# A new issue order, other PSUM banks and other engines for the same 1680 steps of a linear-attention and FFN kernel

## The chip, the cores and the metric

The kernel runs on one core of a Trainium2 chip. The core has a matrix engine (TensorE: PE in the profile, its weight loads PEld), a vector engine (VectorE: DVE), a scalar engine (ScalarE: ACT), GpSimd (POOL) and SyncE (SP). Here POOL and SP mostly issue DMAs, and sixteen DMA engines carry them out. Each engine works through its own instruction stream in order and waits on semaphores for the others. The metric is the device time of one launch in microseconds (us), the median of several runs. Times in the profile count from the first instruction.

## The reference

Inputs are `q`, `k`, `v` of 8 batches x 8 heads x 576 rows x 64, a feature matrix `w_phi` (64x128), and FFN weights `moe_w_in` (512x2048) and `moe_w_out` (2048x512), all float32.

```python
def phi(x):
    proj = np.einsum('bhsd,df->bhsf', x, w_phi)
    proj = proj - np.max(np.abs(proj), axis=-1, keepdims=True)
    return np.concatenate([np.exp(proj), np.exp(-proj)], axis=-1)
q_p, k_p = (phi(q), phi(k))
kv = np.einsum('bhsf,bhsd->bhfd', k_p, v)
z = np.sum(k_p, axis=2)
num = np.einsum('bhsf,bhfd->bhsd', q_p, kv)
den = np.einsum('bhsf,bhf->bhs', q_p, z)[..., None] + 1e-06
attn = num / den
...
h = np.maximum(x @ w_in, 0.0)      # x: attn as 4608 rows of 512
out = h * h @ w_out
```

There is no softmax over positions: each head has a small matrix `kv` (256 x 64), with which every query row is multiplied.

## The kernel before, in words

The work goes batch by batch. For each of the 8 batches the attention makes 576 rows of `x`: 512 of them are one block of the FFN, and the last 64 of all batches together make a ninth block (tile `xS`). The FFN of a block is a first matmul (`F1`, L788: x tile by `win`, 16 groups of four 128x512 matmuls), relu and square (L765 or L767, then L774), and a second matmul (`F2`, L882: by `wout`, four row groups, each in four parts of four matmuls), then a copy out of PSUM (`ot`, L193 or L195) and a store. The attention of the next batch is mixed into the FFN of the present one.

The attention of one batch consists of these steps:
- loads of k, q and v by POOL (L249, L257, L269, L278), which also turn float32 into bf16;
- transposes of k and q into `kT` and `qT`: on PE for batches 0 and 1 (L320), from batch 2 on by a transposing DMA of SP (L331);
- projections `Pk` and `Pq` (L347; 64-row matmuls), their largest magnitude (`Mk` L405, `Mq` L498 or L531) on VectorE, and the exponentials on ScalarE (`kp`, `kn` L411; `qf` L544 or `qpn` L584);
- from batch 3 on the q features are turned by a transposing DMA of SP (`Xf`, L548); before that a matmul `Fq` (L569) makes them turned;
- `V` (L428, VectorE) scales v, `KVs` and `KV` (L450, L462) build kv on PE, `kvc` copies it to SBUF;
- per group of 128 rows: `NA` (L648, PE), `SA` (L660, VectorE, scales the half sum), `NB` (L648 again), `rd` (L670, reciprocal), `xo` (L674, VectorE, into a ring of three buffers), and `Xx` (L708), a transposing DMA of SP that makes the x tile `xT` or `xS` which F1 reads.

The program first makes a plan of 1680 numbered steps. A step is a closure that issues one or several instructions on one engine. The lists at the end of the file then say how the steps are issued:
- `ORDER` is the sequence of all steps. `pin` chains each engine's instructions in that sequence, so each engine does its steps in the order in which they stand there.
- `BASES` gives each of the 377 uses of PSUM its bank (0 to 7). A step that opens a bank waits until all readers of the bank's former use are through.
- `STATES` says for 233 steps (relu, `ot`, `kvc` and some copies in the head) whether they run on their first engine or on the other of VectorE and ScalarE.
- `GATES` makes a load of batches 2 and up wait for a named step.
- `FILL` puts matmuls of zeros (L961, "warm") ahead of a step: its number, then bank and count.

```python
    def arrange(self):
        for op in self.ops:
            if op.alt is not None and STATES[op.group] == "1":
                op.eng, op.occ, op.lat = op.alt
        for g, b in zip(self.banks, BASES):
            g.base = int(b)
        return [self.ops[i] for i in ORDER]
...
        if now[0].seq in GATES:
            dep(i, plan.ops[GATES[now[0].seq]].ins, mybir.DependencyClass.Sync)
```

The costs and slacks in the upper part of the file (`act_cost`, `SLACK`, `LD`) have no effect on what is issued: the four lists and `GATES` alone set it.

Steps that are named below, with their line, and their time in the profiled execution:
- head: 0 and 1 load a first piece of k by ACT's queue, 7 and 8 cast it (L193, L195; 2.84 and 3.56), 2 loads w_phi, 3 and 4 cast it (L230; 3.24 on), 5 sets the identity's tile to zero (L238; 3.10), 11 on POOL makes the identity of it (L913; 3.77), 40 is the first transposes (L320; 4.16), 41 their copy, 42 the first projection; 12 to 39 are loads, 22 to 25 win, 36 to 39 wout
- 358 (last load of batch 2's k), 373 and 374 (its kT and qT, SP L331; 49.91 and 54.54), 266, 275, 284 and 293 (the four x tiles of batch 1, SP L708; from 59.33 on), 292 (xo; 64.02), 297 (NA; 64.77), 482 (first F1 of block 1; 70.86)
- 425 and 604 (Pq), 465 (Fq), 441 to 446 (NA, SA, NB, rd, xo, Xx; 446 at 96.58), 755 (kT of batch 4), 608 (Xf), 455 and 464 (Xx; 103.33 and 106.08), 665 and 669 (F1 of block 2)
- 659 and 661 (NA and NB; 145.5), 838 to 842 (SA, NB, rd, xo, Xx; 842 at 173.16), 1081 (ot; 171.59), 990 and 1002 (Xf), 1137 (kT of batch 6; 181.19), 1022 (Pq), 972 (KVs), 1139 (Pk; 187.81)
- 1028 and 1030 (NA, NB), 1156 (Mk; 206.75), 1033 (Xx; 208.83), 1238 (first F1 of block 5; 214.7)
- 1425 (NB; 280.7), 1427 (xo), 1428 (Xx, the last part of xS; 289.95), 1585 (F1 of the ninth block; 300.8), 1666 to 1673 (last F2, in halves, L846), 1674 and 1675 (their copies), 1676 to 1679 (their stores, by SP and ACT)

Of the kernel before, what the change touches and what calls it, by code (L numbers as in the profile page):

```python
# [108 lines left out]
def kernel(  # L109
# [858 lines left out]
    2, 0, 1, 13, 14, 12, 8, 6, 7, 5, 3, 4, 11, 19, 40, 41, 9, 42, 46, 48, 10, 74, 66, 47, 75, 15, 67, 76, 45, 43, 18,  # L968
    68, 44, 77, 17, 71, 58, 88, 16, 90, 59, 70, 89, 26, 91, 27, 60, 78, 69, 92, 20, 49, 80, 81, 79, 28, 50, 61, 21,
    93, 51, 94, 30, 72, 52, 54, 98, 63, 57, 95, 22, 99, 64, 131, 65, 73, 53, 23, 55, 62, 83, 24, 156, 82, 132, 25,  # L970
    157, 29, 56, 133, 101, 38, 85, 128, 102, 84, 109, 86, 34, 212, 87, 110, 103, 213, 36, 111, 129, 214, 37, 112,
    104, 113, 105, 100, 215, 130, 33, 194, 158, 106, 195, 218, 108, 107, 216, 188, 219, 96, 114, 189, 121, 97, 115,
    134, 217, 122, 200, 206, 135, 116, 123, 207, 124, 159, 117, 125, 201, 136, 118, 126, 160, 190, 137, 127, 119,
    191, 120, 142, 161, 138, 145, 143, 220, 146, 307, 308, 221, 147, 139, 311, 312, 309, 144, 233, 162, 313, 303,
    140, 163, 304, 223, 148, 141, 164, 149, 322, 305, 222, 165, 310, 150, 166, 319, 323, 306, 151, 315, 314, 320,
    152, 196, 316, 198, 321, 167, 317, 153, 197, 325, 154, 199, 318, 328, 168, 326, 169, 155, 324, 170, 174, 329,
    208, 171, 356, 186, 175, 331, 330, 35, 187, 209, 176, 184, 39, 245, 332, 334, 246, 32, 185, 173, 177, 234, 31,
    172, 340, 335, 178, 361, 211, 327, 202, 359, 179, 203, 341, 477, 360, 210, 481, 365, 180, 181, 204, 357, 242,
    336, 346, 225, 243, 224, 355, 205, 485, 358, 247, 342, 347, 236, 363, 182, 267, 226, 276, 362, 268, 352, 183,
    235, 337, 269, 364, 227, 366, 192, 277, 489, 353, 549, 193, 338, 278, 237, 254, 238, 373, 255, 239, 490, 348,  # L980
    244, 248, 241, 258, 240, 249, 228, 259, 229, 230, 270, 260, 231, 374, 285, 333, 343, 271, 232, 339, 261, 344,
    272, 262, 495, 286, 263, 499, 250, 287, 264, 273, 265, 503, 274, 266, 354, 294, 251, 295, 507, 252, 275, 256,
    296, 279, 508, 513, 280, 253, 257, 551, 345, 288, 281, 547, 289, 349, 282, 556, 283, 290, 379, 350, 284, 375,
    553, 382, 517, 291, 376, 744, 531, 292, 377, 367, 381, 293, 297, 535, 370, 298, 378, 369, 380, 521, 552, 299,
    351, 422, 548, 387, 300, 423, 539, 389, 546, 525, 301, 557, 390, 371, 543, 526, 388, 554, 438, 544, 413, 550,
    482, 439, 414, 372, 486, 440, 563, 483, 416, 368, 424, 484, 383, 487, 429, 417, 747, 478, 430, 555, 564, 474,
    488, 431, 384, 740, 492, 475, 479, 476, 391, 504, 395, 392, 385, 500, 493, 404, 505, 518, 406, 501, 302, 494,
    396, 522, 386, 506, 502, 510, 397, 523, 527, 405, 565, 480, 415, 496, 394, 524, 519, 540, 497, 511, 393, 514,
    498, 398, 532, 491, 515, 407, 754, 545, 541, 516, 419, 559, 447, 533, 420, 399, 400, 749, 448, 401, 741, 534,
    408, 449, 582, 512, 739, 409, 403, 402, 410, 562, 583, 536, 411, 737, 421, 412, 432, 520, 585, 668, 561, 433,  # L990
    738, 537, 528, 418, 584, 742, 434, 672, 435, 748, 529, 436, 558, 574, 538, 437, 425, 456, 577, 542, 722, 746,
    426, 457, 560, 575, 726, 934, 428, 458, 441, 730, 442, 743, 576, 530, 443, 604, 444, 427, 734, 445, 607, 446,
    450, 605, 465, 676, 466, 755, 467, 451, 680, 606, 735, 452, 570, 681, 453, 566, 454, 704, 572, 567, 686, 608,
    609, 571, 568, 459, 569, 708, 745, 460, 573, 616, 461, 586, 455, 619, 690, 462, 463, 587, 468, 618, 712, 509,
    469, 464, 578, 617, 470, 580, 694, 620, 471, 472, 716, 581, 628, 579, 640, 631, 698, 736, 621, 589, 665, 630,
    756, 588, 683, 699, 629, 596, 666, 673, 595, 717, 677, 674, 682, 632, 667, 590, 678, 641, 591, 633, 592, 684,
    669, 593, 594, 935, 598, 701, 937, 670, 473, 597, 642, 687, 679, 931, 671, 675, 945, 610, 688, 695, 611, 643,
    689, 691, 752, 685, 696, 612, 943, 702, 705, 613, 692, 614, 750, 765, 703, 706, 599, 936, 652, 693, 600, 767,
    707, 723, 928, 697, 653, 768, 939, 719, 724, 932, 655, 766, 601, 720, 753, 713, 603, 938, 654, 602, 757, 769,
    714, 751, 758, 622, 645, 731, 658, 930, 623, 759, 859, 715, 933, 760, 732, 771, 624, 634, 656, 625, 709, 635,  # L1000
    626, 863, 710, 770, 644, 636, 727, 711, 877, 733, 728, 637, 638, 772, 867, 729, 718, 721, 700, 807, 725, 761,
    615, 881, 764, 885, 809, 639, 762, 871, 808, 947, 763, 889, 872, 646, 810, 895, 647, 890, 795, 773, 797, 627,
# [105 lines left out]
```

## Time and profile before

| what | value |
|---|---|
| median of 3 runs | 345.33 us (344.21 to 345.71) |
| profiled execution: own time | 346.37 us |
| profiled execution: span | 344.6 us |
| granted TensorE clock, mean | 0.998 |
| busy: PE, DVE, ACT, POOL | 333.8, 269.2, 221.6, 95.5 us |
| DMA, mean over the span | 149 GB/s, 51.51 MB |
| matmuls F2 (L882) and F1 (L788), busy | 127.7 and 104.7 us (L788 from `xS`: another 15.3) |
| fillers (L961) | 128 matmuls, 11.1 us busy |

The profiled execution is one run of the program, recorded by the hardware. Its own time is longer than its span by what lies ahead of the first and behind the last recorded instruction. A row of a timeline has the start, the duration, engine, line, operation, the tiles written and read, the shape and the number of instructions; in brackets stands how long the engine was idle before it, and what ended that. "SPq" rows are the issues of DMAs on SP: their duration is that of the issue, and the transfer lands later. Matmuls are pipelined: one of 512 columns takes 379 ns from start to end, but they follow each other every 0.216 us.

### The profile page before, as it was taken

To read this page: it belongs to the slowest core of one execution; us is meant where nothing else is said; L and a number is where in the kernel's file an instruction comes from. 1 tells how busy PE (TensorE), PEld (TensorE's weight loads), DVE (VectorE), ACT (ScalarE), POOL (GpSimd) and SP (SyncE) were. 2 spreads that over 40 slices of the span, in tenths; PEclk is the share of its full clock that TensorE was granted. 3 is DMA by queue.
4 is the path that set the end of the run, shared out by engine and by line. 5 is a ranking of instruction groups with operands and counts; after the bars stand their busy time and mean duration, and the time that the engine had idled before them with its cause. 6 is when DMAs were issued, how large, how long until landed. Compare 5 with 4: busy or idle time off the path is not lost.

```text
span 344.6 us, 8417 instructions
## 1 busy us (share of the span) xinstructions
PE 333.8 (97%) x3371; PEld 189.0 (55%) x3402; DVE 269.2 (78%) x490; ACT 221.6 (64%) x388; POOL 95.5 (28%) x143
## 2 busy tenths in 40 slices
PE   8999999799998999999999999999999999999995
PEld 7789776445554554545545554555555454444443
DVE  5999998799888798888869987798978748861540
ACT  5999996499898787577887896886376201111101
POOL 8760571952910480104604061330000000000000
PEclk9999999999999999999999999999999999999999
DMA  9999999999999999999999999999964631101115
GB/s 135 176 205 202 201 131 157 181 154 210 128 165 195 197 169 197 177 182 185 193 178 178 170 195 168 214 151 171 199 123 92 135 90 54 47 0 62 31 58 126
DMA packets 142935, 51.51 MB, mean 149 GB/s; under 512 B 111472, under 2 KB 138416, under 8 KB 142896
## 3 DMA queue, kind: packets, MB, share of 16 engines
q1 hardware_dynamic: 97488, 32.35, 51.8%
q0 software_dynamic: 44960, 18.23, 46.3%
q8 instruction: 26, 0.43, 0.6%
q10 hardware_dynamic: 448, 0.39, 0.4%
q14 instruction: 13, 0.11, 0.1%
HBM read 36.73 MB, written 9.44 MB: 134 GB/s over the span
## 4 chain that ended last, share of the span: by engine, by line
PE 86%; DVE 5%; DMA 5%; issue 2%; ACT 1%; POOL 1%; SPq 0%; DVEq 0%; POOLq 0%
PE psum L882 31%; PE psum L788 30%; PE psum L648 5%; PE psum L462 5%; PE psum L347 5%; DMA xT<-xo 3%; PE psum L827 2%; DMA kT<-xk 2%; DVE mk L405 2%; PE psum L813 1%; PE psum L799 1%; PE psum L569 1%; PE psum L846 1%; PE psum L320 1%; PE psum L450 1%
## 5 line engine op out<-in xcount | busy, mean ns | idle before, releaser
L882 PE MATMUL psum<-wout,h 128*128 128x512 bf16 x529 | 127.7, 379 | 1.7 <-issue 0.3
L788 PE MATMUL psum<-xT,win 128*128 128x512 bf16 x448 | 104.7, 379 | 1.0 <-DMA xT<-xo 1.0
L765 ACT ACTIVATE hr<-psum 128x512 bf16<-128x512 f32 x95 | 54.9, 601 | 47.9 <-DVE h L774 28.8
L882 PEld LDWEIGHTS <-h 128*128 128x128 bf16 x560 | 51.3, 98 | 56.7 <-issue 0.3
L788 PEld LDWEIGHTS <-win 128*128 128x128 bf16 x512 | 47.4, 98 | 53.6 <-DMA xT<-xo 1.4
L774 DVE TENSOR_TENSOR h<-hr 128x512 bf16<-128x512 bf16 x144 | 56.6, 415 | 10.6 <-ACT hr L765 10.2
L544 ACT ACTIVATE qf<-psum 128x1024 bf16<-128x1024 f32 (+1 forms) x50 | 45.6, 937 | 8.6 <-PE psum L347 6.1
L405 DVE TENSOR_REDUCE mk<-psum 128x8 f32<-128x1024 f32 (+1 forms) x38 | 42.3, 1119 | 4.0 <-ACT kn L411 1.9
L411 ACT ACTIVATE kn<-psum 128x1024 bf16<-128x1024 f32 (+1 forms) x38 | 36.0, 947 | 12.8 <-PE psum L347 11.1
L411 ACT ACTIVATE kp<-psum 128x1024 bf16<-128x1024 f32 (+1 forms) x38 | 35.6, 948 | 8.2 <-PE psum L347 6.6
L767 DVE TENSOR_SCALAR hr<-psum 128x512 bf16<-128x512 f32 x49 | 33.1, 684 | 9.0 <-PE psum L788 8.2
L660 DVE TENSOR_TENSOR psum<-psum,en 128x520 f32<-128x520 f32 (+1 forms) x39 | 27.2, 703 | 10.4 <-PE psum L648 6.1
L648 PEld LDWEIGHTS <-qpn 128*128 128x128 bf16 x624 | 27.0, 97 | 15.0 <-issue 3.3
L269 POOL DMA_DIRECT2D xq<-in_q_dram x24 | 17.3, 727 | 56.3 <-issue 14.0
L531 DVE TENSOR_REDUCE mq<-psum 128x8 f32<-128x1024 f32 (+1 forms) x25 | 27.8, 1113 | 6.5 <-PE psum L347 3.9
L648 PE MATMUL psum<-kv,qpn 128*128 128x65 bf16 x624 | 30.2, 193 | 1.9 <-DVE xo L674 1.7
L249 POOL DMA_DIRECT2D xk<-in_k_dram x27 | 19.9, 740 | 30.6 <-ACT en L508 15.3
L584 ACT ACTIVATE qpn<-psum 128x1024 bf16<-128x1024 f32 (+1 forms) x30 | 27.0, 956 | 1.8 <-PE psum L569 1.8
L674 DVE TENSOR_TENSOR xo<-psum,rden 128x512 bf16<-128x512 f32 (+1 forms) x39 | 26.3, 684 | 2.4 <-DMA xT<-xo 1.8
L195 ACT ACTIVATE ot<-psum 128x512 f32<-128x512 f32 x18 | 10.8, 598 | 25.7 <-PE psum L882 25.7
L249 POOL DMA_DIRECT2D xv<-in_v_dram x27 | 19.8, 740 | 14.6 <-PE psum L788 11.7
L428 DVE TENSOR_TENSOR va<-xv,va 128x1280 bf16<-128x1280 bf16 (+2 forms) x34 | 23.2, 710 | 0.0
(79 smaller groups left out, 352.8 us busy)
## 6 DMA issues: line engine op xcount, KB each, us to landing
out_dram<-ot SPq DMA_DIRECT2D x32, 256.0 KB, 3.0
xk<-in_k_dram POOLq DMA_DIRECT2D x25, 128.0 KB, 5.1
xq<-in_q_dram POOLq DMA_DIRECT2D x24, 128.0 KB, 5.1
xv<-in_v_dram POOLq DMA_DIRECT2D x24, 128.0 KB, 5.1
win<-in_moe_w_in_dram POOLq DMA_DIRECT2D x4, 512.0 KB, 10.7
wout<-in_moe_w_out_dram POOLq DMA_DIRECT2D x4, 512.0 KB, 15.5
xq<-in_q_dram POOLq DMA_DIRECT2D x4, 256.0 KB, 6.1
out_dram<-ot SPq DMA_DIRECT2D x6, 128.0 KB, 2.4
```

The costliest lines, as they stand in the source:

```text
L249: pin(nc.gpsimd.dma_start(out=x[:, m0 + a * 512 : m0 + z * 512].rearrange("p (h x) -> p h x", x=4 * D), in_=src[b][2 * a : 2 * z, 0:512, : ...
L405: pin(nc.vector.tensor_reduce(out=mk_view(g), in_=ps2(pj)[:, :, : n * Fd].rearrange("p e (i f) -> p e i f", f=Fd), axis=AX.X, op=ALU.max, ...
L411: pin(nc.scalar.activation(out=dst[slot][:, :, :n, :].rearrange("p e i f -> p e (i f)"), in_=ps2(pj)[:, :, : n * Fd], func=ACT.Exp, scale= ...
L531: pin(nc.vector.tensor_reduce(out=mqb[:, c, :, :n], in_=ps2(pj)[:, :, : n * Fd].rearrange("p e (i f) -> p e i f", f=Fd), axis=AX.X, op=ALU ...
L544: pin(nc.scalar.activation(out=o, in_=i_, func=ACT.Exp, scale=sgn))
L648: pin(nc.tensor.matmul(out=o[:, u // 4, u % 4 * D1 : (u % 4 + 1) * D1], lhsT=qpn[slot][:, sg * half + u * m : sg * half + u * m + P], rhs= ...
L660: pin(nc.vector.tensor_tensor(out=o, in0=o, in1=enb[:m, c, :].rearrange("t (b h) -> t b h", b=2).to_broadcast([m, 2, 4, D1]), op=ALU.mult))
L765: pin(nc.scalar.activation(out=hr[sl], in_=ps1(g), func=ACT.Relu))
L767: pin(nc.vector.tensor_scalar(out=hr[sl], in0=ps1(g), scalar1=0.0, scalar2=None, op0=ALU.max))
L774: pin(nc.vector.tensor_tensor(out=dst, in0=i_, in1=i_, op=ALU.mult))
L788: pin(nc.tensor.matmul(out=o, lhsT=win[mc // 4][:, kc, mc % 4 * P : (mc % 4 + 1) * P], rhs=x, start=(kc == 0), stop=(kc == KC - 1)))
L882: pin(nc.tensor.matmul(out=ps1(g), lhsT=h2[c % 2][mc // 4][:, mc % 4, tt * P : (tt + 1) * P], rhs=wout[mc // 4][:, mc % 4, :], start=(mc = ...
```

## The change

The plan of steps, their code and `GATES` stay as they are. `ORDER`, `BASES`, `STATES` and `FILL` get other contents:
- `ORDER`: the steps are permuted, mostly by a few places. SP's sequence (113 DMAs) is the same in both. POOL's differs only among the loads 18 to 38: the loads of win come in the order 24, 23, 22, 25 rather than 22, 23, 24, 25, those of wout as 36, 37, 38, 39 rather than 38, 36, 37, 39, and 29 goes behind 36; some small loads change places.
- `STATES`: 78 of 233 steps change their engine, 42 from VectorE to ScalarE and 36 the other way (43 relus, 18 copies `ot`, 15 copies `kvc`, and one each of `kcast` and `Cxq`).
- `BASES`: 314 of 377 uses of PSUM get another bank.
- `FILL`: 89 filling matmuls instead of 128; the 23 ahead of step 101, the 9 ahead of 51 and others go, some are spread otherwise.

The diff, with the lines in which the steps named above stand:

```diff
--- before.py
+++ after.py
 ORDER = [
-    2, 0, 1, 13, 14, 12, 8, 6, 7, 5, 3, 4, 11, 19, 40, 41, 9, 42, 46, 48, 10, 74, 66, 47, 75, 15, 67, 76, 45, 43, 18,
...
-    93, 51, 94, 30, 72, 52, 54, 98, 63, 57, 95, 22, 99, 64, 131, 65, 73, 53, 23, 55, 62, 83, 24, 156, 82, 132, 25,
-    157, 29, 56, 133, 101, 38, 85, 128, 102, 84, 109, 86, 34, 212, 87, 110, 103, 213, 36, 111, 129, 214, 37, 112,
...
-    553, 382, 517, 291, 376, 744, 531, 292, 377, 367, 381, 293, 297, 535, 370, 298, 378, 369, 380, 521, 552, 299,
...
-    426, 457, 560, 575, 726, 934, 428, 458, 441, 730, 442, 743, 576, 530, 443, 604, 444, 427, 734, 445, 607, 446,
-    450, 605, 465, 676, 466, 755, 467, 451, 680, 606, 735, 452, 570, 681, 453, 566, 454, 704, 572, 567, 686, 608,
...
-    469, 464, 578, 617, 470, 580, 694, 620, 471, 472, 716, 581, 628, 579, 640, 631, 698, 736, 621, 589, 665, 630,
...
-    669, 593, 594, 935, 598, 701, 937, 670, 473, 597, 642, 687, 679, 931, 671, 675, 945, 610, 688, 695, 611, 643,
...
-    648, 1128, 913, 649, 650, 929, 798, 899, 774, 651, 777, 917, 796, 786, 657, 811, 776, 659, 903, 660, 775, 921,
-    779, 778, 907, 780, 799, 925, 788, 831, 926, 781, 661, 782, 832, 873, 783, 946, 860, 908, 784, 800, 833, 785,
...
-    977, 988, 1080, 991, 962, 839, 1081, 1062, 840, 841, 1104, 1063, 842, 848, 998, 956, 1001, 952, 1108, 953, 990,
...
-    1060, 1047, 980, 968, 849, 1126, 851, 1051, 1048, 1130, 971, 1013, 852, 1116, 1127, 1049, 1052, 1134, 1065, 1117,
...
-    1139, 1022, 1074, 972, 1025, 973, 979, 974, 1091, 1023, 976, 1142, 1069, 1082, 975, 1140, 1024, 1100, 1095, 1075,
...
-    1424, 1530, 1425, 1566, 1534, 1570, 1516, 1501, 1517, 1519, 1502, 1426, 1552, 1535, 1503, 1513, 1427, 1520, 1509,
-    1514, 1553, 1505, 1510, 1515, 1554, 1571, 1531, 1506, 1428, 1511, 1541, 1507, 1532, 1536, 1523, 1518, 1555, 1524,
...
-    1561, 1568, 1612, 1569, 1529, 1577, 1546, 1585, 1578, 1547, 1573, 1557, 1579, 1563, 1574, 1596, 1586, 1616, 1564,
...
-    1647, 1657, 1664, 1648, 1666, 1649, 1668, 1650, 1670, 1651, 1658, 1672, 1667, 1674, 1669, 1671, 1673, 1676, 1677,
...
+    2, 0, 1, 13, 14, 7, 12, 8, 6, 3, 4, 5, 11, 19, 40, 41, 9, 42, 47, 48, 10, 66, 74, 46, 67, 15, 75, 45, 68, 43, 17,
...
+    51, 20, 72, 52, 73, 94, 30, 54, 63, 95, 57, 131, 24, 99, 56, 53, 23, 64, 55, 65, 82, 81, 156, 132, 22, 128, 157,
+    25, 62, 36, 83, 101, 133, 34, 85, 109, 102, 84, 212, 29, 87, 110, 86, 103, 213, 111, 37, 129, 214, 158, 113, 38,
...
+    517, 377, 291, 292, 744, 382, 531, 376, 293, 367, 381, 297, 521, 370, 298, 378, 369, 380, 535, 552, 299, 351,
...
+    457, 575, 441, 560, 726, 458, 934, 730, 442, 743, 576, 443, 604, 444, 445, 607, 465, 676, 446, 466, 605, 450,
...
+    578, 586, 690, 617, 580, 620, 470, 717, 694, 471, 609, 472, 581, 628, 640, 631, 698, 579, 736, 669, 756, 629,
+    595, 665, 670, 699, 673, 666, 596, 630, 598, 677, 682, 621, 588, 642, 632, 683, 667, 678, 671, 590, 641, 674,
...
+    903, 907, 799, 659, 831, 660, 781, 782, 661, 783, 662, 788, 925, 785, 873, 832, 784, 908, 946, 860, 663, 834,
...
+    839, 988, 1062, 840, 841, 1081, 956, 1063, 842, 998, 952, 1000, 1104, 953, 990, 977, 1086, 1001, 957, 1090, 979,
...
+    1134, 852, 1125, 1048, 1073, 853, 1053, 1013, 1136, 854, 1077, 1061, 855, 1074, 1065, 1078, 1049, 1014, 1022,
+    1066, 972, 1139, 973, 1142, 1067, 974, 1025, 1140, 1069, 1141, 1023, 1091, 1082, 1015, 1070, 1100, 976, 1087,
...
+    1548, 1516, 1552, 1517, 1509, 1501, 1510, 1553, 1511, 1570, 1502, 1554, 1423, 1505, 1424, 1513, 1425, 1514, 1527,
+    1426, 1506, 1541, 1528, 1507, 1537, 1503, 1427, 1519, 1428, 1559, 1520, 1534, 1521, 1545, 1535, 1529, 1523, 1536,
+    1515, 1518, 1538, 1531, 1539, 1546, 1585, 1547, 1555, 1524, 1571, 1639, 1556, 1525, 1532, 1594, 1542, 1533, 1549,
...
+    1657, 1664, 1667, 1647, 1648, 1666, 1649, 1668, 1650, 1670, 1651, 1658, 1672, 1669, 1674, 1671, 1673, 1676, 1677,
...
 ]
 BASES = (
-    '1455230076225145762234566476424460160675235573406256700052456706030226636000051065454425544316464174'
...
+    '6577674402105660622234544776027640120422067175676462540072457642204004626222261062736606141516020635'
...
 )
 STATES = (
-    '0100000001011000110001110010000100000000100011110000100100001010000000101000100000000000001011010001'
-    '1010110000001000010000010001110100000000001111000000000100011000011010001011011000101110111101101011'
-    '111111100001100010101111001011011'
+    '1100000001011000100001110011010100000000100011100100110000001010000000010110000100000000001000000100'
+    '0100101101000000011010011011010000010100000111010001000100000000010110000100001101000000000000111111'
+    '101000110110110110111110101110000'
 )
...
 FILL = {
-    40: (0, 26), 42: (0, 11), 74: (0, 5), 76: (0, 7), 58: (0, 10), 60: (4, 16), 92: (4, 1), 51: (6, 9), 131: (4, 8),
-    156: (3, 2), 101: (3, 23), 188: (4, 3), 134: (2, 1), 142: (5, 6),
+    40: (0, 26), 42: (0, 11), 66: (0, 5), 68: (2, 7), 58: (4, 10), 60: (7, 7), 92: (7, 7), 131: (1, 7), 156: (7, 2),
+    109: (4, 1), 142: (5, 6),
 }
```

6 lines of the change are left out of this document (3 added, 3 removed), and 130 rows, old and new, of the table ORDER.

## The prediction

> **What bounds the kernel now.** I read the page first, then TensorE's waits, then busy time by stretches of the span, and last the timelines of PE, DVE and SP around each place where PE stood idle.
>
> ```profile
> span 344.6 us, 8417 instructions
> PE 333.8 (97%) x3371; PEld 189.0 (55%) x3402; DVE 269.2 (78%) x490; ACT 221.6 (64%) x388; POOL 95.5 (28%) x143
> PEclk9999999999999999999999999999999999999999
> DMA  9999999999999999999999999999964631101115
> ```
>
> PE is busy 97% of the span at full clock, and the DMA engines are 90% busy or more in the first 29 of 40 slices (up to 250 us). A new order of the same steps can win no more than PE's idle time. By stretches (columns: length, then PE, PEld, DVE, ACT, POOL busy):
>
> ```profile
> 27.00:62.70 35.70, 35.38 (x531) 26.70 (x533) 32.62 (x64) 30.42 (x56) 14.89 (x23) 1.00 1.32 174
> 62.70:70.80 8.10, 6.38 (x63) 3.25 (x62) 5.88 (x8) 4.33 (x7) 7.37 (x11) 1.00 1.51 167
> 70.80:111.00 40.20, 38.94 (x405) 20.29 (x404) 35.80 (x59) 36.84 (x62) 14.95 (x22) 1.00 1.22 168
> 111.00:188.00 77.00, 76.14 (x739) 39.90 (x746) 64.76 (x114) 57.72 (x100) 25.69 (x38) 1.00 1.24 185
> ```
>
> Idle PE between 27 and 188 us is 0.32 + 1.72 + 1.26 + 0.86 us. Three waits hold most of it; these are PE's rows:
>
> ```profile
> 64.77 0.40 PE L648 MATMUL psum<-kv,qpn 128*128 128x65 bf16 x8 [1.67 <-DVE xo L674]
> ...
> 110.79 1.47 PE L788 MATMUL psum<-xT,win 128*128 128x512 bf16 x6 [0.95 <-DMA xT<-xo]
> ...
> 187.81 0.29 PE L347 MATMUL psum<-wphi,kT 64*128 64x128 bf16 x4 [0.39 <-DMA kT<-xk]
> ```
>
> All three are late transposing DMAs of SP's queue. The first goes through VectorE:
>
> ```profile
> 49.91 4.33 SPq L331 DMA_TRANSPOSE kT<-xk  x1
> 54.54 4.74 SPq L331 DMA_TRANSPOSE qT<-xq  x1
> 59.33 6.61 SPq L708 DMA_TRANSPOSE xT<-xo  x4
> ...
> 64.02 0.69 DVE L674 TENSOR_TENSOR xo<-psum,rden 128x512 bf16<-128x512 f32 x1 [1.83 <-DMA xT<-xo]
> ```
>
> SP issues kT, then qT, then four x tiles, one behind the other. The xo of step 292 reuses a buffer that step 266 is still transposing; that landed at 63.93, so 292 runs at 64.02, its bank comes free, and PE's step 297 starts at 64.77. The second wait has the same queue behind it, issuing without a pause:
>
> ```profile
> 96.58 1.54 SPq L708 DMA_TRANSPOSE xT<-xo  x1
> 98.42 3.38 SPq L331 DMA_TRANSPOSE kT<-xk  x1
> 101.90 1.33 SPq L548 DMA_TRANSPOSE qpn<-qf  x1
> 103.33 2.04 SPq L708 DMA_TRANSPOSE xT<-xo  x1
> 105.42 0.57 SPq L900 DMA_DIRECT2D out_dram<-ot  x1
> 106.08 1.22 SPq L708 DMA_TRANSPOSE xT<-xo  x1
> ```
>
> The last of these (step 464) landed at 110.74, and PE went on at 110.79.
>
> **The change part by part.** GATES, SP's own sequence (113 DMAs) and, after the head, POOL's sequence are identical in both lists. I therefore counted, for each wait, which PE steps stand ahead of it in the old and in the new ORDER.
>
> Head, 0 to 27 us. The memset of the identity (step 5) goes behind the two casts of w_phi (3, 4) on VectorE, and the first cast of xk goes to ScalarE. Rows: memset 0.11 at 3.10, casts 0.95 for the two from 3.24, POOL's select 0.33 at 3.77, first transposes 4.16. Upper end: the casts take as long as now, end at 4.1, memset 4.2, select 4.6, transposes 4.65: 0.5 late. Lower end: the casts, which ran beside POOL's issue (3.00 to 3.73) and select, take no more than the 0.30 of the larger cast at 2.84; memset done at 3.85, transposes at about 4.25: 0.1 late. I take 0.3, between rows that are equally near. Behind the select on POOL stand load 19 and all later loads, behind the transposes step 41 on VectorE and the first projection; VectorE is busy 10.00 of the 10 us from 10 to 20 and 9.86 of the next 10, so the delay is carried on. The other way, weight load 24 goes ahead of 22 and 23: step 311 started at 27.75, 0.21 after its weights landed at 27.54, so up to 0.3 may come back. Of the fillers 39 go (23 of them take 1.46 at 15.25, 0.056 apart), 39 x 0.056 = 2.2 us of PE, but they stand where PE waits for VectorE: nothing. The head's sum is -0.3 to +0.5.
>
> What covers it: PE's steps ahead of 297 are the same set in both lists, and so are those ahead of 482, the first matmul of the next block (70.86, on the landing of step 293 at 70.82). Step 266 could not be issued before SP was through with qT at 59.3, and kT started 0.08 after its last load (step 358) landed at 49.83. That load waited for an earlier landing before it was issued (POOL at 46.05), with the DMA engines full; the same loads come before it in the new list. So 64.77 stays, PE's 1.67 of idle time there grows or shrinks, and the head counts 0. If this cover is gone, it counts its own -0.3 to +0.5.
>
> 70.8 to 111 us. Fq 465 is drawn up to Pq 604, which makes one stretch of 64-row matmuls of two. A stretch costs its switch: at 207.14 twelve matmuls of 0.216 end at 209.73, three projections of 0.23 follow, and the next matmul comes at 210.60, so 0.87 - 0.69 = 0.18. But step 464 lands when SP's queue is through, counted from the xo of step 445 at 96.55, and the PE steps from NB 443 to the first F1 (669, formerly 665) are the same set. The 0.18 lengthens the idle 0.95: counted 0. If no wait stood there it would be -0.18.
>
> 111 to 188 us. The copy ot 1081 (0.69 at 171.59) goes from VectorE to ScalarE; rd 840 and xo 841 stood behind it, and x-tile step 842 waited for them on SP (free 171.4, issued 173.16). It can be issued up to 0.65 sooner, and 990, 1002 and kT 1137 behind it; Pk 1139 also moves behind Pq 1022 and KVs 972. Bounds: 0 if the queue gives the time back, -0.39 if the wait goes. Nearest row: SP issued all three without a pause, so I take -0.39. Next behind it is step 1022, which stands ready. Against it, NB 661 moves up to 1.08 us of PE work behind its NA 659 (4.06 before), while the pair 441/443 shows 1.37 from NA's start to SA's end (93.75 to 95.12). Bounds 0 to +0.3; I take +0.3, since nothing stands still there. Pairs under 1.5 us number 15 before and 11 in the new list; the others either were as short or lie ahead of a wait.
>
> 188 to 285 us. The same set of PE steps stands ahead of F1 1238, and DVE's mk 1156 (1.21 from 206.75) holds x tile 1033 back as before, so NB 1030's later place is covered: 0. The 78 steps that change between VectorE and ScalarE (42 to ScalarE, 36 back) lighten VectorE by six, and the rows name it ahead of no idle time of PE after 66 us; I count 0, with the bound under the rivals.
>
> 285 us to the end. F1 1585 moves to 8.0 us behind NB 1425 (20.1 before). It needs rd 0.2, a relu 0.69, two squares of 0.42, xo 0.68 and a landing of 2.6 (step 1428 took that from 289.95), some 6.3 with the matmul before the relu: 1.7 are left, 0. F2h 1667 (4 x 0.056) goes ahead of 1672, so ScalarE's last copy is 0.22 late and its queue's last store 0.1: +0.1, bounds 0 to +0.22.
>
> Sum: 0 + 0 - 0.39 + 0.3 + 0 + 0.1 = 0.0. The profiled execution took 346.37 (span 344.6 and 1.8 around it), 1.0 above the median of 345.33; I put the sum on the median: 345.3.
>
> [...] Row: PE stood idle for 1.67 us at 63 and the stretch keeps a clock of 1.00; where the 23 fillers at 15.25 go, 1.4 us of idle time is left, shorter than that. [...]
>
> **The rivals.**
> Faster: the first wait goes. The loads of the head are reordered, and if step 358 landed 1.7 earlier, the whole 1.67 would be won, with the 0.39: 345.3 - 1.7 = 343.6 or, with what lies behind it, 343.2. For it: POOL waits for landings (1.22 at 46.05). Against it: the bytes before are the same and the DMA row is full.
> Slower: banks handed back too late. Place: 111 to 285 us, where PE has no idle time to give. PE steps that open a bank under 1.5 us of PE work after its last user number 29 in the old list, 33 in the new one. A short one needs a read of 0.60 to 0.70 and some 0.3 around it, or 1.2 behind a reduction, so one costs up to 0.5. From four at the full price it decides (over 1.7): 345.3 + 2.0 = 347.3. For it: 314 banks change. Against it: under 2.5 us there are 126 before and 122 now.
> [...]
>
> **How the numbers follow.** Half a percent, 1.7 us, is about what a measurement of this kernel can tell from no change. No change (forecast): 0.56, its own range 344.3 to 346.3. First wait gone or more: 0.18. Banks: 0.20. Clock: 0.06. So faster 0.18, same 0.56, slower 0.26. Predicted 345.3. The range reaches past the outer rivals by 0.6 and 0.9, less than the three runs are apart (1.5): from 342.6 to 348.2.
>
> **What would show it.** Right: PE's wait for xo near 64.8 and for xT near 110.8 at the same times, one larger or smaller by what the head gives; kT's wait near 187.8 gone; first transposes at 4.2 to 4.7. Wrong: those two waits at other times, new waits of PE on DVE or ACT between 111 and 285, or a clock under 1.00 between 15 and 25 us.

## The result, and the profile after

The changed kernel takes 348.9 us (median of 4 runs, 347.5 to 351.9) against 345.5 for the kernel before on the same chip: ratio 1.0117, 95% interval 1.0083 to 1.0152. Measured again later, with 12 runs of its own, it took 347.6 against 345.5, ratio 1.0059 (1.0032 to 1.0086). It is slower by 2.1 to 3.4 us. Forecast was no change, 345.3. Ratios leave out a few disturbed runs; medians and counts below are over all runs of a kernel.

The profiled execution is the mildest of the first four: own time 347.5, 1.1 over the profiled one of before. From its page, the span, TensorE and the row of the granted clock:

```profile
span 345.7 us, 8332 instructions
PE 332.8 (96%) x3333; PEld 187.5 (54%) x3363; DVE 264.6 (77%) x484; ACT 225.7 (65%) x394; POOL 95.5 (28%) x143
PEclk9989999999999999999999999999999999999999
```

TensorE is busy 1.0 us less than before, and the third slice (17 to 26 us) no longer has the full clock. The stretches shown before (length, then PE, PEld, DVE, ACT, POOL busy):

```profile
27.00:62.70 35.70, 35.31 (x534) 26.78 (x539) 33.69 (x68) 29.51 (x53) 13.24 (x20) 1.00 1.28 167
62.70:70.80 8.10, 7.44 (x71) 3.91 (x72) 6.30 (x12) 5.27 (x7) 6.67 (x11) 1.00 1.34 149
70.80:111.00 40.20, 39.70 (x411) 20.63 (x414) 35.29 (x57) 36.55 (x62) 17.29 (x26) 1.00 1.28 176
111.00:188.00 77.00, 76.27 (x735) 40.00 (x742) 65.55 (x114) 58.72 (x103) 25.70 (x38) 1.00 1.24 183
```

Idle TensorE there is 0.39 + 0.66 + 0.50 + 0.73 us, 1.9 less than before (4.2). The two waits on which the forecast rested shrank, so the time went somewhere else: into the head. The same four stretches of 3.41 us, cut where the clock changed; first the changed kernel (the last three columns are the clock, the DMA share and GB/s):

```profile
10.51:13.92 3.41, 2.44 (x38) 2.18 (x38) 3.31 (x6) 3.41 (x7) 3.19 (x5) 1.00 1.56 188
13.92:17.34 3.42, 1.95 (x21) 1.25 (x20) 3.42 (x5) 3.42 (x10) 1.78 (x3) 1.00 1.78 178
17.34:20.75 3.41, 3.41 (x47) 2.53 (x45) 3.34 (x7) 2.80 (x4) 3.41 (x6) 0.50 1.33 202
20.75:24.16 3.41, 3.01 (x80) 2.63 (x78) 2.74 (x6) 2.64 (x9) 1.55 (x3) 1.00 1.24 208
```

then the kernel before, with one more stretch, that of its long wait at 63 us:

```profile
10.51:13.92 3.41, 3.14 (x42) 2.29 (x42) 3.41 (x7) 3.41 (x12) 3.25 (x5) 1.00 1.53 179
13.92:17.34 3.42, 3.14 (x38) 2.18 (x37) 3.42 (x5) 3.42 (x7) 1.29 (x3) 1.00 1.76 178
17.34:20.75 3.41, 3.41 (x101) 3.26 (x100) 3.41 (x7) 3.29 (x9) 3.41 (x6) 1.00 1.35 203
20.75:24.16 3.41, 3.15 (x57) 2.34 (x54) 3.27 (x10) 3.31 (x7) 1.51 (x3) 1.00 1.24 207
63.15:66.56 3.41, 1.79 (x16) 0.97 (x16) 1.99 (x3) 1.07 (x2) 3.41 (x6) 1.00 1.52 153
```

Without the 23 fillers TensorE is busy 1.95 of 3.42 us from 13.92 on, and the clock falls to half for the next 3.41 us, where 47 matmuls run instead of 101 (the steps are not quite the same). The KV matmuls of that stretch and of the next, from TensorE's timeline of the changed kernel, show it in their distance: 0.11 us for two, then 0.06:

```profile
19.10 0.30 PE L462 MATMUL psum<-va,kn 128*128 128x65 bf16 x2
19.21 0.30 PE L462 MATMUL psum<-va,kp 128*128 128x65 bf16 x2
...
21.49 0.22 PE L462 MATMUL psum<-va,kn 128*128 128x65 bf16 x2
21.55 0.22 PE L462 MATMUL psum<-va,kp 128*128 128x65 bf16 x2
```

A stretch of 3.41 us at half speed takes 3.41 / 2 / 345 = 0.005 off the mean clock of a run, so the mean clock counts them: the first four runs of the changed kernel had 0.994 (347.5 us), 0.990 and 0.990 (348.9), 0.984 (351.9), that is one, two and three stretches. The two waits of before, in TensorE's rows of the changed kernel, and the third:

```profile
65.59 0.40 PE L648 MATMUL psum<-kv,qpn 128*128 128x65 bf16 x8 [0.61 <-DVE xo L674]
...
110.36 2.32 PE L788 MATMUL psum<-xT,win 128*128 128x512 bf16 x10
...
189.28 0.28 PE L347 MATMUL psum<-wphi,kT 64*128 64x128 bf16 x4 [0.85 <-DMA kT<-xk]
```

The wait for xo is 0.61 instead of 1.67, that for the x tile is gone, that for kT is 0.85 instead of 0.39. How late TensorE is, as the start of a step's first matmul less its start in the profiled execution of before (worked out from TensorE's rows; all these steps have the same steps ahead of them in both orders):

| step | before, us | changed | held by fillers (e6) | held by fillers (r13) | old head, new rest (e4) | thin old head, new rest (e7) |
|---|---|---|---|---|---|---|
| 212 | 17.98 | +0.59 | +0.46 | -0.26 | -0.07 | +0.83 |
| 162 | 28.69 | +1.57 | +0.80 | +0.07 | +0.02 | +1.85 |
| 192 | 47.28 | +2.13 | +1.38 | +0.63 | +0.02 | +1.85 |
| 482 | 70.86 | +0.83 | -0.69 | -1.43 | -1.79 | +0.04 |
| 628 | 107.81 | +1.12 | -0.40 | -1.15 | -1.79 | +0.03 |
| 705 | 119.93 | -0.01 | 0.00 | -0.76 | -2.48 | +3.25 |
| 843 | 161.53 | +0.56 | +0.29 | -0.29 | -1.89 | +3.49 |
| 973 | 188.37 | +1.13 | -0.17 | -0.75 | -2.35 | +3.04 |
| 1238 | 214.92 | +0.98 | -0.32 | -0.90 | -2.50 | +2.88 |

Some matmul records are missing in the executions of before, changed and r13, so a start can be off by 0.1 or 0.2. Two losses of the changed kernel stand in the first three rows. Behind step 212 runs the slow stretch: at step 214, 1.3 us of work further on, the changed kernel is 1.57 late and e6, at full clock, 0.80. And from step 162 to 192 both lose another 0.56 to 0.58, with the clock at full in both.

### The profile page after: what moved, and what is told of

Its sections match the earlier page's. It is cut to its first block, busy times and chain, and to the rows that moved or that the text cites. A ratio compares the mean times of both kernels' runs of the same rounds, so it can differ in the third digit from the quotient of the medians.

```text
span 345.7 us, 8332 instructions
## 1 busy us (share of the span) xinstructions
PE 332.8 (96%) x3333; PEld 187.5 (54%) x3363; DVE 264.6 (77%) x484; ACT 225.7 (65%) x394; POOL 95.5 (28%) x143
## 4 chain that ended last, share of the span: by engine, by line
PE 84%; DMA 5%; ACT 3%; DVE 3%; POOL 2%; issue 2%; SPq 0%; POOLq 0%; DVEq 0%
PE psum L882 31%; PE psum L788 29%; PE psum L648 5%; PE psum L347 5%; PE psum L462 5%; DMA kT<-xk 2%; PE psum L827 2%; DMA xv<-in_v_dram 2%; DMA xT<-xo 1%; PE psum L569 1%; PE psum L799 1%; PE psum L846 1%; ACT qf L544 1%; PE psum L813 1%; ACT kn L411 1%
## 5 line engine op out<-in xcount | busy, mean ns | idle before, releaser
L788 PE MATMUL psum<-xT,win 128*128 128x512 bf16 x448 | 106.3, 379 | 0.3 <-ACT qf L544 0.2
L765 ACT ACTIVATE hr<-psum 128x512 bf16<-128x512 f32 x98 | 57.0, 600 | 56.6 <-PE psum L788 48.4
L544 ACT ACTIVATE qf<-psum 128x1024 bf16<-128x1024 f32 (+1 forms) x50 | 46.1, 939 | 7.2 <-PE psum L347 2.7
L411 ACT ACTIVATE kn<-psum 128x1024 bf16<-128x1024 f32 (+1 forms) x38 | 35.6, 945 | 7.9 <-PE psum L347 6.0
L411 ACT ACTIVATE kp<-psum 128x1024 bf16<-128x1024 f32 (+1 forms) x38 | 35.8, 948 | 4.5 <-PE psum L347 3.7
L767 DVE TENSOR_SCALAR hr<-psum 128x512 bf16<-128x512 f32 x46 | 31.1, 685 | 5.6 <-PE psum L788 4.1
L195 ACT ACTIVATE ot<-psum 128x512 f32<-128x512 f32 x24 | 14.3, 598 | 20.4 <-PE psum L882 20.3
(78 smaller groups left out, 347.9 us busy)
```

What stands on the lines that cost most here:

```text
L411: pin(nc.scalar.activation(out=dst[slot][:, :, :n, :].rearrange("p e i f -> p e (i f)"), in_=ps2(pj)[:, :, : n * Fd], func=ACT.Exp, scale= ...
L544: pin(nc.scalar.activation(out=o, in_=i_, func=ACT.Exp, scale=sgn))
L765: pin(nc.scalar.activation(out=hr[sl], in_=ps1(g), func=ACT.Relu))
L767: pin(nc.vector.tensor_scalar(out=hr[sl], in0=ps1(g), scalar1=0.0, scalar2=None, op0=ALU.max))
L788: pin(nc.tensor.matmul(out=o, lhsT=win[mc // 4][:, kc, mc % 4 * P : (mc % 4 + 1) * P], rhs=x, start=(kc == 0), stop=(kc == KC - 1)))
```

## The experiments

All kernels, in us. "Full" are the runs at a mean clock of 0.998 or more (no stretch at half speed in the work), "fallen" the others, each with its median and number of runs.

| kernel | median | full | fallen | ratio to before (95%) |
|---|---|---|---|---|
| before | 345.3 | 345.2 (116) | 349.4 (8) | |
| changed, both measurements | 347.9 | 345.2 (1) | 348.0 (15) | 1.0117 and 1.0059 |
| e2 changed, refilled | 348.18 | 347.6 (4) | 349.1 (2) | 1.0070 (1.0042 to 1.0098) |
| e3 before, without 23 and 9 fillers | 346.21 | 345.3 (3) | 346.4 (9) | 1.0005 (0.998 to 1.003) |
| e4 and r14 old head, new rest | 344.84 | 344.8 (24) | none | 0.9979 and 0.9989 |
| e5 new head, old rest | 346.87 | 345.0 (3) | 347.3 (9) | 1.0032 (1.0008 to 1.0056) |
| e6 changed, filled | 346.41 | 346.4 (12) | none | 1.0022 (0.9992 to 1.0051) |
| r13 changed, filled otherwise | 346.26 | 346.3 (12) | none | 1.0032 (1.0007 to 1.0057) |
| e7 thin old head, new rest | 348.74 | 344.6 (1) | 349.1 (11) | 1.0076 (1.0043 to 1.0109) |
| e9 before, without 9 | 344.81 | 344.8 (11) | 345.8 (1) | 0.9990 (0.9966 to 1.0015) |
| e10 before, without 23 | 346.93 | 344.1 (1) | 347.3 (11) | 1.0032 (0.9997 to 1.0067) |
| r10 changed, fillers at 111 | 348.89 | none | 348.9 (7) | 1.0084 (1.0054 to 1.0114) |
| r11 e7, fillers at 111 | 346.72 | 344.8 (3) | 347.0 (9) | 1.0040 (1.0013 to 1.0068) |
| r12 before, fillers at 111 | 347.90 | 347.0 (7) | 348.8 (5) | 1.0041 (1.0011 to 1.0072) |
| r15 e4 without 9 | 345.50 | 345.5 (12) | none | 1.0017 (1.0006 to 1.0029) |

### Filling the head again (e2), and thinning that of before (e3)

```diff
 FILL = {                                   # e2, in the changed kernel
-    ... 60: (7, 7), ... 156: (7, 2),
+    ... 60: (7, 12), ... 156: (6, 9), 51: (7, 9), 101: (4, 23),
```

> The changed kernel with the idle places of the head filled again: 23 matmuls of zeros ahead of step 101, 9 ahead of 51, 9 ahead of 156, 5 more ahead of 60; nothing else. Theory A (the clock): the changed kernel's runs carry mean clocks of 0.994, 0.990, 0.990 and 0.984 at spans of 345.7 to 350.2, about one more stretch of 3.41 us at half speed for each step down; with the places filled every run has 0.997 or 0.998, the slow stretch at 17.3 to 20.8 us is gone, and what is left is the 1.2 us that the profiled execution loses between 147 and 188 us: 346.2 to 346.8, with a spread under 1.5. Theory B (the order, banks and engines behind the head carry the loss, the clock is covered): 348 to 349, whatever the clock. Theory C (both are small beside DMA landings of the head that come later): 348 to 349 and clock 0.998.

```diff
 FILL = {                                   # e3, in the kernel before
-    ... 51: (6, 9), ... 101: (3, 23),
```

> The kernel before without its 23 matmuls of zeros ahead of step 101 and the 9 ahead of 51; nothing else. Theory A: the clock falls to half for 3.41 us or more somewhere between 14 and 24 us, mean clock 0.984 to 0.994 in most runs; one such stretch makes the work of 3.41 us take 1.4 to 1.7 us longer, which the idle 1.67 us at 63 covers, two or more come through: median 346.0 to 348.5, and runs far apart. Theories B and C: TensorE is idle in those places anyway, 345.5 with clock 0.998.

e2 was a poor filling. At 348.18 it misses what theory A forecast and lies where B and C had it, but it cannot speak for them: its fillers waited themselves, 0.86 us for a reader of bank 6 ahead of step 156 and 0.39 for one of bank 4 ahead of 101. Four of its six runs kept the clock and still took 347.6. It says that a filler needs a bank that is free, and no more on the theories. e3 bears theory A out: taking fillers away from an idle engine lets the clock fall in 9 of 12 runs (mean clocks of 0.988 to 0.993), and inside one and the same kernel those take 346.4 against 345.3. Against the kernel before, e3 as a whole is not measurably slower (1.0005, 0.998 to 1.003).

### Head and rest apart (e4, e5)

Both kernels are put together from the two lists; the head is the first 306 steps of the old order, up to about 48 us of TensorE. Banks and engines go with the steps.

```python
head = set(OLD_ORDER[:306])
ORDER = [s for s in OLD_ORDER if s in head] + [s for s in NEW_ORDER if s not in head]   # e4, FILL of before
ORDER = [s for s in NEW_ORDER if s in head] + [s for s in OLD_ORDER if s not in head]   # e5, FILL of the change
```

> The first 306 steps in the order of the kernel before (TensorE up to about 48 us), with its banks, engines and fillers; all later steps as in the changed kernel. Theory A: clock 0.998. In the changed kernel's profiled execution TensorE is 0.2 ahead at 120 us and 1.0 late at the end, so the new rest costs about 1.1: 346.2 to 346.8, with new waits near 155 (a bank, 0.3) and near 188 (kT, 0.9). Theory B (rest carries all): 348.5 to 349. Were it the head alone: 344.9 to 345.5.

> The other half: the first 306 steps as in the changed kernel, with its thin filling, all later ones as in the kernel before. Theory A: mean clock 0.984 to 0.994; with one slow stretch TensorE is 0.8 late at 66 us and the wait for an x tile at 110.8 takes that up, 345.5 to 346; with two or three 347 to 349; median 346 to 348. Theory B: 345.3, whatever the clock. Theory C: 347 to 348 at any clock.

e4 came out at 344.93: the new rest does not cost the 1.1 us that I had read off the profiled execution, it costs nothing that can be measured. Reading a loss between 120 us and the end off one pair of executions was wrong. e5, with the new head alone, is slower, and again by its clock: 347.3 where it fell and 345.0 where it did not. Theory B falls, and so does C, which wanted 347 at any clock. The windows of e5's profiled execution show a fall that lasts two stretches:

```profile
13.36:16.77 3.41, 2.39 (x29) 1.64 (x27) 3.31 (x6) 3.41 (x10) 1.75 (x4) 1.00 1.72 180
16.77:20.18 3.41, 2.77 (x31) 1.72 (x31) 3.22 (x8) 3.27 (x4) 3.41 (x5) 0.50 1.42 201
20.18:23.60 3.42, 3.42 (x65) 3.23 (x62) 2.22 (x2) 1.21 (x7) 1.76 (x3) 0.50 1.25 209
```

In the slow stretch from 16.77 on TensorE still had 0.64 us without work, and the clock did not come back; it came back behind the stretch that was full.

### The clock held in the changed kernel (e6), and a thin old head before the new rest (e7)

```diff
 FILL = {                                   # e6, in the changed kernel
-    ... 156: (7, 2),
+    ... 156: (7, 8), 51: (7, 8), 128: (7, 20),
```

> The changed kernel with 34 more matmuls of zeros, placed where the bank written is free by the trace: 8 ahead of step 51, 6 more ahead of 156, 20 ahead of 128 (all into bank 7, which step 128 opens itself; nothing reads 128 before 19.6 us). Nothing else is changed. Theory A (the clock, now with its size): clock 0.998 or more in nearly every run, no stretch at half speed. Runs at full clock of the two half-changed kernels had medians near 345 (345.1 with the new head, 344.9 with the new rest), so 344.5 to 345.5, 3.5 under the changed kernel. Theory B (new head and new rest together lose time whatever the clock): 347 or more at clock 0.998.

> Old head without its 23 fillers ahead of step 101 and its 9 ahead of 51, and the new rest. Clock 0.988 to 0.994 in three runs of four. If the new rest has less slack against a late head than the old one, 347 to 348 in the runs with a low clock (the old rest with this head: 346.4 in those, 345.3 in the others); if it has the same, 345.5 to 346 (0.7 under, as at full clock).

e6 holds the clock in all 12 runs (0.998 or more). From its windows:

```profile
12.64:16.05 3.41, 2.75 (x37) 1.90 (x34) 3.19 (x6) 3.36 (x12) 2.27 (x3) 1.00 1.64 184
16.05:19.47 3.42, 3.42 (x61) 2.65 (x60) 3.32 (x7) 3.42 (x5) 2.43 (x4) 1.00 1.57 194
```

It is worth 1.2 to 2.5 us (347.6 and 348.9 to 346.4), not 3.5: 1.2 us over the 345.2 of the kernel before stay with the clock at full. By the ratio (1.0022, 0.9992 to 1.0051) this remainder is at the edge of what can be told; r13 below confirms it. e7 is the surprise: an old head, thinned, costs 1.1 us at a fallen clock before the old rest and some 3 to 4 before the new one (its fallen runs have a median of 349.1, the seven of them under 350 us one of 347.9; its one full run took 344.6). Its profiled execution falls twice, in the head and again at 113.5 us:

```profile
14.54:17.96 3.42, 1.65 (x16) 0.89 (x16) 3.42 (x5) 3.42 (x7) 2.07 (x4) 1.00 1.68 164
17.96:21.37 3.41, 3.41 (x58) 3.22 (x57) 2.66 (x6) 2.06 (x4) 3.41 (x5) 0.50 1.32 203
110.11:113.53 3.42, 1.18 (x6) 0.59 (x7) 0.77 (x1) 0.54 (x2) 0.00 (x0) 1.00 1.17 160
113.53:116.94 3.41, 3.41 (x10) 1.23 (x9) 2.92 (x6) 2.59 (x6) 0.00 (x0) 0.50 0.93 209
```

Ahead of the second fall stands this wait, in TensorE's rows of e7:

```profile
112.35 2.06 PE L788 MATMUL psum<-xT,win 128*128 128x512 bf16 x7 [2.48 <-DMA xT<-xo]
```

It is the wait for the x tile that the forecast had as 0.95 and as cover. At 2.48 us it costs itself and then half of the 3.41 us behind it: between steps 628 and 705 e7 loses 3.2 us on the kernel before, which waited 0.95 there.

### Which fillers (e9, e10)

Each takes one entry out of the kernel before.

```diff
-    51: (6, 9),                            # e9
-    101: (3, 23),                          # e10
```

> The kernel before without only the 9 fillers ahead of step 51 (at 10.8 us). Theory A1 (what counts is how much the matrix engine streams in a window of 3.41 us, at least a little over half): counted from the rows (columns at 0.216 us per 512), windows that begin at 10 to 11.5 us would stream 0.53 to 0.60 of their length, against 0.41 to 0.52 ahead of the four falls seen so far and 0.56 or more where the clock stayed: the clock falls in no more than 2 runs of 12, median 345.6. Theory A2 (any stall of 0.5 us or more counts): it falls in most runs, 346.4.

> The kernel before without only the 23 fillers ahead of step 101 (at 15.25 us). Theory A1: windows that begin at 13 to 15.5 us stream 0.30 to 0.53 of their length, and nearly every position of the windows has one such: the clock falls in 8 to 12 runs of 12, mean clock 0.988 to 0.994 there, and those take 1.0 to 1.5 more than the ones at full clock; median 346.2. If the clock needed a window with no work at all, it would stay at 0.998 in all, 345.6.

Both as theory A1 had it in the clocks: it fell in 1 of 12 runs without the 9, and in 11 of 12 without the 23. So it is the 23 that hold it; the 9 can go for nothing. The price of e10's falls was higher than expected, 347.3 against one run at 344.1, though against the kernel before e10 as a whole is not clear of noise (1.0032, 0.9997 to 1.0067). Where it falls was seen in one execution only, and that one kept the clock in the head and fell at 111.6 us, behind a wait of 2.4 us for the x tile:

```profile
108.20:111.61 3.41, 1.00 (x6) 0.50 (x6) 1.83 (x2) 1.57 (x4) 0.00 (x0) 1.00 0.79 119
111.61:115.02 3.41, 3.41 (x10) 1.18 (x9) 0.74 (x2) 0.87 (x3) 0.00 (x0) 0.50 1.14 263
```

### Are there falls at 111 us in the changed kernel? (r9 to r12)

r9 is the changed kernel once more; the others put 20 fillers ahead of the first F1 of block 2, into the bank that it opens.

```diff
+    669: (7, 20),                          # r10 in the changed kernel, r11 in e7
+    665: (6, 20),                          # r12 in the kernel before
```

> The changed kernel once more, for the spread of its clock. Each stretch of 3.41 us at half speed takes 0.005 off the mean clock of a run. Theory D (the clock falls at two places: in the head, and near 111 us, where TensorE waits for an x tile): clocks of 0.984 to 0.995 in every run, median 348 to 349.5, a run with one more stretch 1.5 to 3 us above one with one less.

> The changed kernel with 20 matmuls of zeros ahead of step 669, the first F1 of block 2, where TensorE waits for the x tile (into the bank that 669 opens itself, free 1.6 us earlier); the head stays thin. Theory D: the falls near 111 us go, those of the head stay: no run under 0.988, and the median falls by about 1 to 347.5 to 348; where nobody waits the 20 cost up to 1.1. Theory A alone (all falls lie in the head): the same clocks as the changed kernel, and 0 to 1.1 us more time.

> Old head without its 23 and 9 fillers, new rest, and 20 matmuls of zeros ahead of step 669. Without the 20 its runs had clocks of 0.985 to 0.995 and a median of 348.74, and the profiled one fell at 18.0 us and again at 113.5 us behind a wait of 2.5 us. Theory D: the second fall goes; clocks of 0.988 to 0.995, 346 to 347. Rival E (the new rest loses the time in other waits): 348.7 or more.

> The kernel before, complete, with 20 matmuls of zeros ahead of step 665, its first F1 of block 2 (wait there 0.95 us in the profiled run). Theory D: its rare runs of 0.993 to 0.995, at 348.8 to 350.1 where the others have 345, go; the median stays within 0.5 of 345.3, since most of the 1.1 us lies in the wait. Rival: those runs stay, so their falls lie elsewhere.

r9: 347.62, a little under its forecast, and 11 of 12 runs between 0.985 and 0.995; its one run at full clock took 345.2. r10 speaks against theory D for the changed kernel: clocks of 0.988 to 0.994 as without the fillers, and 348.9, 1.0 over the median of the 16 runs without them. Its falls lie in the head, and the profiled executions of r9 and r10 show them there, each two stretches long (15.2 to 22.0 and 16.8 to 23.7 us). r11 points to theory D in e7 but does not show it: 346.72 instead of 348.74 and no run under 0.988 (e7 had two), but the intervals of the two ratios overlap (1.0013 to 1.0068 and 1.0043 to 1.0109), and 5 of its 12 runs still have 0.990 or less, where e7 had 6. r12 is a miss: the fillers made the kernel before slower by 2.4 us, twice what they hold, and two of its runs still fell to 0.995 (three more had 0.997); in its profiled execution the 20 took the place of the wait and cost nothing, and the time went at 66 us, where the wait for xo was 2.9. What the rise of the median comes from stays open, and the falls of before, 8 of 124 runs, are not traced to a place.

### What is left at full clock (r13 to r15)

```diff
 FILL = {                                   # r13, in the changed kernel
-    ... 131: (1, 7),
+    ... 131: (1, 11), 51: (7, 8), 128: (7, 18),
```

> The changed kernel with 8 fillers ahead of step 51, 4 more ahead of 131 and 18 ahead of 128, none added ahead of 156, where those of the earlier filling waited 0.47 us. Clock 0.998 or more in nearly all runs. If the earlier filling's 1.0 us over the kernel before was the price of its own waits: 345.0 to 345.5. If the new head loses it by its order: 346.2 to 346.6 again.

> Old head with its fillers, new rest, once more. If the new rest gains by itself: 344.6 to 345.0 against 345.4 for the kernel before, ratio 0.997 to 0.999; if it is worth nothing: 345.4, ratio 1.000.

> As the one before, without the 9 fillers ahead of step 51, without which the kernel before kept its clock in 11 of 12 runs. If fillers in idle places cost nothing: 344.7 to 345.2, clock 0.998 or more in at least 10 of 12 runs.

r13 gives 346.26 with the clock held in 12 of 12, so e6's 346.4 was not only the price of its fillers' waits. In both, head and rest of the change together, TensorE waits for the x tile near 111 again, 1.4 us in e6 and 1.3 in r13; from the lists of TensorE's waits of e6, and then of e4 (waiting engine and line, what for, us in total, times, longest):

```profile
PE psum L788 <- DMA xT<-xo: 1.4, 1, 1.4
```

```profile
PE psum L788 <- DMA xT<-xo: 0.3, 1, 0.3
```

The length of that wait is not by itself the loss: the kernel before has 0.95 there, and e9, at 344.8, has 1.4. What goes with the time is when the tile lands (step 464). In the seven executions at full clock in which TensorE waits for it and no filler was added there, the span ends 233.3 to 234.0 us behind that landing (before 110.74 and 344.6, e4 108.26 and 342.3, r13 109.98 and 343.9, e6 110.75 and 344.4; the others are e9, r14 and r15). In e6 it lands 2.5 and in r13 1.7 us later than in e4, and that has two parts. First, the transfer of step 446, with which this stretch of SP's queue begins, is issued 1.4 and 0.65 later: that is how late TensorE comes out of the new head (1.38 and 0.63 at step 192), and in neither of the two executions is there a wait for xo near 64.8 that could take it up. Second, the queue needs 1.1 longer from there to the landing (14.7 against 13.6). Over the 17 executions it needed 12.7 to 16.0, so the second part is not shown to belong to the order. Of the first, 0.55 to 0.58 us belong to the new head, its order, banks or engines: TensorE loses them between steps 162 and 192, behind all fillers of the head, in all seven executions with the new head, at any clock, and in none of the nine with the old one other than before itself (0.00 there). What else the new head costs at full clock, and what its fillers take, is not separated; the changed kernel's one run at full clock without added fillers took 345.2.

r14 repeats e4: 344.57, ratio 0.9989 (0.9958 to 1.0019). Old head and new rest, 344.84 over 24 runs, is with e9 (344.81) the best found; it beats the changed kernel by 3 us, but not measurably the kernel before. r15 lost 0.9 to r14 where nothing was expected. Its TensorE waits 0.93 us at 12.42 for the exponential of L411, but that only takes the place of the fillers: in r14, with them, the same step starts at 12.46. Near 111 it waits 0.8 where r14 waits 0.3; whether that has to do with the missing 9 fillers, one execution does not tell.

## Why the prediction was wrong, point by point

**The step that failed: "Of the fillers 39 go ... but they stand where PE waits for VectorE: nothing."** They cost nothing to leave out as work, but they held the clock. I compared the longest idle time that would be left, 1.4 us, with one of 1.67 us behind which the clock had stayed. The profile of after has idle times of no more than 0.39, 0.21 and 0.87 us in the stretch ahead of the fall. What the runs showed in place of "nothing": the clock fell in 15 of 16 runs of the changed kernel, and with fillers put back where their bank was free (e6, r13) in none of 24, which is worth 1.2 to 2.5 of the 2.1 to 3.4 us. Why the clock fell behind 1.95 of 3.42 us busy is not tested. What differs from the wait at 63 us, with 1.79 of 3.41 us busy at a clock of 1.00, is with what the stretch is filled: there stand eight 512-column matmuls, in the head sixteen 64-row projections, with 0.87 us of idle time behind them. By the count of the last section 0.57 of the stretch at 63 us was streamed, and 0.22 of the one in the head.

**The slow stretches: how long, and where.** In the windows above each is 3.41 or 3.42 us long, and there are one or two in a row. Where they begin differs between executions of one program: in the changed kernel the clock fell at 17.34 us in one profiled execution and at 15.19 in the other (r9), and over all of them the falls in the head begin anywhere from there to 18.70 (e3). The number of falls differs between runs of one kernel too (mean clocks of 0.984 to 0.994 in the first four of the changed one). TensorE was by no means idle for the whole stretch ahead of the fall: it was busy 1.95 of the 3.42 us, with short idle times of 0.39, 0.21 and 0.87 us between groups of matmuls, and I had not weighed that place.

**The clock's chance.** A clock under 1.00 between 15 and 25 us came, 0.50 from 17.34 to 20.75 us of the profiled execution, and 0.06 was far too low for what came in 15 of 16 runs. It was my estimate, with no run behind it: the trace of before has no fall within its work (mean clock 0.998). Most runs have two slow stretches or more, by their mean clocks (0.990 or less in 13 of the 16). With the clock held the kernel still takes 346.3 to 346.4, so the one slow stretch is worth some 1.1 us in the profiled run of 347.5, and the rest does not come from the clock.

**The head's own -0.3 to +0.5.** The identity was hardly late: first transposes at 4.20 (4.16 before), the lower edge of the 4.2 to 4.7 forecast. But with the clock held TensorE is 1.38 (e6) or 0.63 (r13) late at 47 us. 0.57 of it arises behind the head, between 28.7 and 47.3 us, a stretch for which the prediction had no term at all; 0.28 of that stands ahead of step 164, an NB, which had NA 148 right ahead of it and now has the matmuls of step 304 between them. I counted the whole as covered by the wait for xo, and that wait is absent in e6 and r13.

**"So 64.77 stays."** It did not. I had the anchor fixed by landings; the load that it starts from moved with the head. POOL's rows, before and then after (step 355 is the first of the two):

```profile
46.05 1.41 POOL L249 DMA_DIRECT2D xk<-in_k_dram  x2 [1.22 <-DMA xq<-in_q_dram]
```

```profile
46.92 1.43 POOL L249 DMA_DIRECT2D xk<-in_k_dram  x2 [1.93 <-DMA xq<-in_q_dram]
```

From there the 0.87 runs through SP (kT 50.80, qT 55.27, x tiles 60.09, where before had 49.91, 54.54 and 59.33) to the xo of step 292 at 64.84 instead of 64.02. So of 2.07 us of lateness at 60 us 1.24 were taken up, and 0.83 came through. Nor is the 1.67 to be counted on: in e3, e4 and e5 step 266 landed 0.2 to 3.7 us earlier than the 63.93 of before, and the wait for xo does not appear. These are other kernels, but r9 is the changed one again, and has 0.3 there instead of 0.61.

**70.8 to 111, "0", and the wait for the x tile.** Step 464 landed at 110.66 (110.74 before), as argued, and the later TensorE used up the wait. But it does not stand still either: it landed between 107.8 and 114.2 in the other profiled executions, and the wait was between nothing and 2.5 us.

**The 0.39 of kT.** Wrong: 0.85 instead of gone. The copy 1081 went to ScalarE as said, but the sum SA 838 came 1.03 later on VectorE (170.97 against 169.94), behind one more reduction, so xo 841 and x tile 842 were issued 0.20 later (173.36), not 0.65 earlier. I had moved one copy off the queue and not read what else moved onto it. In r9, the same kernel again, the wait is absent, as it is in e4, r14 and e5 under either rest, so that it is no property of the edit.

**NB 661, the tail, 188 to 285.** The +0.3 did not come: TensorE is 0.01 ahead at 135.2 and 0.02 ahead at 146.8. From 188 to 215 us it gained 0.15 and nothing after (0 forecast). At 340.5 us it is as late as at 334.7 (0.99), and the span is 1.14 longer, so that the part behind TensorE cost 0.15, where +0.1 was forecast. These are too small to matter.

**The banks as a rival** is not what happened: between 111 and 285 us, kT aside, the one new wait of TensorE for another engine is 0.21 at 154.47, where an F1 waits for the exponential of L544, a reader of PSUM; from 147.6 to 161.5 us TensorE falls back by 0.58 in all. In e4, with all of the new banks from 50 us on, that wait is absent, and e4 and r14 take 344.8. In the head the banks count in another way: the two that e2 used for fillers ahead of steps 156 and 101 were not free in time.

## What to carry to other kernels

Here matmuls of zeros in idle places held the clock: it fell in 8 of 124 runs of the kernel before and in 11 of 12 without the 23. Before such matmuls are taken out, work out how much the matrix engine streams in every stretch of the length that the clock's record shows (3.41 us here), wherever it begins, and not only how long its longest pause is: here the clock fell behind streamed shares of 0.38 or less, and of the idle times ahead of the changed kernel's fall the longest was 0.87 us. The mean clock of each run counts the slow stretches (0.005 each here) and splits the runs of a noisy kernel into groups that can be compared. A wait that is to cover a loss should be looked for in several executions: over these kernels the two that the forecast rested on were anywhere between nothing and 2.9 us. And a stretch without waits needs a term of its own: 0.57 us were lost in one that the sum left out.

## What the runs showed of the hardware

I counted, in the 17 profiled executions, the work that TensorE streamed in each stretch of 3.41 us of the clock's record: 0.216 us for 512 columns, and half of that per column for all 64-row matmuls; a matmul counts in the stretch in which it starts. The half is my choice: 16 of 64 rows and 128 columns take 0.62 us at 109.40 in r12 and 16 of full height 1.05 at 28.94 in the kernel before, but 16 of 64 rows also take 1.05 at 15.27 in the changed kernel. (In e7 from 110.11 on: six matmuls of 512 columns, 1.30 of 3.41 us, 0.38.) The clock fell 9 times in the work, each time behind a stretch of 0.38 or less, and once more in each execution where the work runs out at the end (0.52 from 343 to 344 us in the kernel before, 0.51 from 345 us on in the changed one). In over 1600 other stretches it stayed, and only a few of those lie under 0.40, the lowest at 0.36. The two falls that the table leaves out, in the heads of r9 and r10, lie at 0.33 and 0.30:

| stretch from | kernel | streamed | clock next |
|---|---|---|---|
| 14.54 | e7 | 0.19 | half |
| 13.92 | changed | 0.22 | half |
| 13.36 | e5 | 0.30 | half |
| 14.36 | e2 | 0.33 | half |
| 15.28 | e3 | 0.34 | half |
| 108.20 | e10 | 0.32 | half |
| 110.11 | e7 | 0.38 | half |
| 12.62 | e10 | 0.36 | full |
| 11.13 | e7 | 0.41 | full |
| 11.95 | before | 0.45 | full |
| 63.15 | before | 0.57 | full |

Counted by columns alone the two groups overlap (it fell at up to 0.52, and stayed at 0.38, 0.49 and 0.52 with matmuls of full height). The share was fitted after the fact, and some matmul records are missing, so it is a description of these traces and no tested rule. At half clock it came back behind stretches in which TensorE was busy 0.94 or more of the time (all 3.41 us from 17.34 on in the changed kernel), and not behind those of 0.81 (2.77 of 3.41 us from 16.77 on, e5), 0.82 (r10) and 0.87 (2.96 of 3.42 us from 15.19 on, r9).
